# Block products for half of layer 2's w_out: seven products for eight in four of its eight units

## The chip, the cores and the metric

One core of a Trainium2 chip runs the whole program in one launch. The metric is the device time of that program in microseconds; the kernel before has a median of 2010.13 us over three runs (2009.96 to 2010.89).

## The reference, cut to what matters

Three stages in float32 over 12160 tokens (2 sequences of 6080) of width 256; both feed-forward layers widen to 2048.

```
f = lb + (1 - lb) * sigmoid(f_logit)             # gate
h[t] = f[t] * h[t-1] + (1 - f[t]) * x[t]         # scan over a sequence, y[t] = h[t]
a  = y @ w_in1;  g = a - tanh(a);         z   = g @ w_out1     # layer 1
b  = z @ w_in2;  g = max(0.01 * b, b);    out = g @ w_out2     # layer 2
```

## The kernel before, in words

**Tiles.** Tokens are cut into 12 chunks of 1024 (the last has 896), each chunk into two halves of H = 512, which are the columns of every matmul. Features lie on the 128 partitions. The work is a list of 24 items (`items`): an item is one layer over one chunk, and from item 1 on the layers take turns, so that odd items are layer 1 (of chunk c) and even items from 2 on are layer 2 (of chunk c - 1). An item has 8 units; a unit is 256 of the 2048 hidden features, as two blocks of 128.

**Precision.** Every operand is split in two float32r parts, hi (a rounded copy, made by ScalarE) and lo (the rest, by VectorE's subtraction), and every 128x128 block product is three matmuls of 512 columns: hi by hi, hi by lo, lo by hi.

**First product of a unit** (w_in, `product`, L453). The unit's 2x2 block product would take eight block products; from item 3 on it takes seven, of sums of blocks (`S1` to `S4` of the weights, `T1` to `T4` of the tokens), 21 matmuls in the PSUM banks b1, c11 and c12. Two PSUM additions on VectorE (L834, c12; L852, c22) and two copies on ScalarE (L799, c11; L821, s5) join the parts, and `act` (L481) reads the four results c11, c12, c21, c22 out to SBUF as g. In layer 1 `shrink` (L490) then subtracts the tanh. `make_forms` (L408) builds the seven token forms of an item and their hi and lo parts during the item before.

**Second product** (w_out, `emit_B`, L515). Each of the four g blocks is split (`hi`, L495, and `lo`, L500) and multiplied with two 128-wide column blocks of w_out, six matmuls for each g block and 24 for a unit, into the four banks `acc`, where all 8 units of an item add up. `sums` gives the two banks of half n; two items in turn use them crosswise.

**Order.** All engine queues are written out by hand (`manual_schedule`). The main loop (L792) takes one unit per step: in step t it issues the first product of unit t and, between its parts, the second product of unit t - 1 (`prev`), so an item's last unit is finished in step 0 of the next item. Each engine works through its queue in this order; an instruction that waits holds up all behind it on its engine. Other jobs are put into slots, four to a step (`put`, `work`): slot 4k + j of an item is place j in its step k. Such jobs are the token loads (`load_tokens`, eight DMAs of SyncE for one half of the features k), the scan of a chunk (`front`, transposes, gate and scan pieces of 256 tokens on VectorE, tanh on ScalarE; k = 0 and k = 1), the forms of the next item and `evacuate` (L527), which reads the finished sums of the item before: layer 1 by ScalarE copies (z), layer 2 by VectorE transposes straight out of PSUM (o) and four DMAs each. The slots of a layer-2 item hold both halves of the scan for the layer-1 item after it, and that item's forms; those of a layer-1 item, from its step 2 on, the forms of the next layer-2 item.

**Weights** are converted in the first items and kept in DRAM; `stream_a` (L263, two steps ahead) and `stream_b` (L272, one step ahead) bring each unit's blocks back through SyncE's queue. The pool `conv` holds the conversion's buffers, among them those of `sums_in` (L193), which adds up w_in's block sums.

Of the kernel before, what the change touches and what calls it, by code (L numbers as in the profile page):

```python
# [20 lines left out]
def tile_gated_scan_two_ffn(  # L21
# [39 lines left out]
    NPLAIN = 3  # L61
    assert [l for l, _ in items[:NPLAIN]] == [0, 0, 1]

# [8 lines left out]
    op = ctx.enter_context(tc.tile_pool(name="op", bufs=2))  # L72
# [11 lines left out]
    wb_d = [[dram.tile([P, 2, 2, DM], F32, name=f"wb{l}{u}") for u in range(NU)] for l in range(2)]  # L84

# [158 lines left out]
    wa, wb = {}, {}  # L244

    def wa_tile(key):
        wa[key] = wp.tile([P, 2, 7, P], F32R, tag="wa", name="wa")
        return wa[key]

# [13 lines left out]
    def stream_a(t):  # L263

        it, u = divmod(t, NU)
        if 0 < it < len(items):
            n = 4 if it < NPLAIN else 7
            w = wa_tile(t)[:, :, 0:n]
            nc.sync.dma_start(w.bitcast(F32), wa_d[items[it][0]][u][:, :, 0:4] if n == 4 else
                              wa_d[items[it][0]][u][:, :, 1:8])  # L270

    def stream_b(t):  # L272
        it, u = divmod(t, NU)
        if 0 < it < len(items):
            nc.sync.dma_start(wb_tile(t).bitcast(F32), wb_d[items[it][0]][u])
# [132 lines left out]
    def make_forms(it):  # L408
# [24 lines left out]
        def sub(i, a, b):  # L433
            s[i] = sp.tile([P, H], F32, tag="t", bufs=3, name="t")
# [7 lines left out]
        for i, make in (  # L442
# [8 lines left out]
            jobs += [lambda i=i: split_hi(i), lambda i=i: split_lo(i)]  # L451
        return jobs


    def product(u, bank, w, v, start=False):
        it, l, h, wt = u["it"], u["l"], u["h"], u["wa"]
# [37 lines left out]

    def hi(u, name):  # L495
        h = u["h"]
        gh = u["hi", name] = gp.tile([P, H], F32R, tag="gh", name="gh")
        nc.scalar.copy(gh[:, :h], u["g", name][:, :h])  # L498

    def lo(u, name):  # L500
        h = u["h"]
        gl = u["lo", name] = gp.tile([P, H], F32R, tag="gl", name="gl")
# [12 lines left out]
    def emit_B(u, name):  # L515
# [4 lines left out]
        first = (it, n) not in begun  # L520
        begun.add((it, n))
        for e in range(2):
            es = slice(e * P, (e + 1) * P)
            for i, (s, v) in enumerate(((0, gh), (0, gl), (1, gh))):
# [3 lines left out]
                )  # L528

    def evacuate(it, n):  # L530
# [10 lines left out]

        def o(e):
            if it == NPLAIN - 1 and n == 0:
                t = sp.tile([P, H], F32, tag="t", bufs=3, name="o")
            else:
                t = op.tile([P, H], F32, tag="o", name="o")
            nc.vector.transpose(t[:, :h], bank[e][:, :h])  # L547
# [65 lines left out]

    with tc.manual_schedule():
# [277 lines left out]
```

## Time and profile before

| | |
|---|---|
| median of the timed runs | 2010.13 us (2009.96 to 2010.89) |
| profiled execution, first to last instruction | 2007.9 us (the page gives no other time for it) |
| TensorE busy | 1982.2 us, 99% |
| VectorE busy | 1421.5 us, 71% |
| ScalarE busy | 1207.0 us, 60% |
| bytes moved by DMA | 345.68 MB, mean 172 GB/s |

TensorE is PE for matmuls and PEld for the weight loads beside them; VectorE is DVE, ScalarE is ACT, SyncE's DMA queue is SPq. L numbers are lines of the kernel. Times in rows of a timeline are microseconds from the first instruction. The duration of a matmul row is modelled and overlaps that of the next one, so the start-to-start distance tells the pace. A group of rows gives the busy time, the mean duration in ns, then the idle time of the engine ahead of these instructions and what ended it.

### The profile page before, as it was taken

Reading aid. Unit: us, or ns where it says so; the run is one execution under the profiler, and the core shown is the slowest. Engines: PE = TensorE matmul, PEld = TensorE weight load, DVE = VectorE, ACT = ScalarE, POOL = GpSimd, SP = SyncE. Lnnn points to the kernel's source line nnn. Section 1 sums busy time; section 2 is a strip of 40 time slices with the busy share of each in tenths; the row PEclk is TensorE's granted clock in tenths of the full one; section 3 lists DMA queues with packets and bytes.
Section 4 is the critical chain, followed back from the end, with each engine's and each line's share of the span. In section 5 each row is a group of like instructions: output and inputs, shape, how many; then the busy total and the mean of one; then the engine's idle time right before and its main releaser. Section 6 shows DMA issues by size and latency. Waiting matters only on the chain.

```text
span 2007.9 us, 24511 instructions
## 1 busy us (share of the span) xinstructions
PE 1982.2 (99%) x8776; PEld 1648.0 (82%) x8776; DVE 1421.5 (71%) x2259; ACT 1207.0 (60%) x2199; POOL 0.7 (0%) x6
## 2 busy tenths in 40 slices
PE   6999999999999999999999999999999999999998
PEld 4888887888888888888888888888888888889888
DVE  7989978866776775775776677677577577666443
ACT  4556656665665665666566566666566656666554
POOL 0000000000000000000000000000000000000000
PEclk8999999999999999999999999999999999999999
DMA  5556778845645554463563554555446356354352
GB/s 200 156 147 231 261 267 266 265 165 165 178 152 165 165 165 131 159 180 142 165 186 144 165 174 157 165 162 162 138 159 180 143 164 181 145 167 172 141 168 87
DMA packets 369818, 345.68 MB, mean 172 GB/s; under 512 B 273568, under 2 KB 277536, under 8 KB 369696
## 3 DMA queue, kind: packets, MB, share of 16 engines
q1 hardware_dynamic: 368048, 342.02, 52.8%
q10 hardware_dynamic: 1648, 2.10, 0.3%
q8 instruction: 69, 1.13, 0.2%
q14 instruction: 53, 0.43, 0.1%
HBM read 306.45 MB, written 37.62 MB: 171 GB/s over the span
## 4 chain that ended last, share of the span: by engine, by line
PE 94%; DVE 3%; ACT 1%; DMA 1%; issue 1%; SPq 0%; ACTq 0%; DVEq 0%
PE acc L525 49%; PE b L459 22%; PE c L459 17%; PE b L475 5%; PE c L525 1%; PE c L475 1%; DVE g L493 1%; DVE gl L503 1%; DMA raw<-in_moe_w_out_dram 0%; DVE y L346 0%; DMA rawf<-in_f_logit_dram 0%; DVE o L547 0%; DVE b L127 0%; DVE raw L138 0%; ACT g L485 0%
## 5 line engine op out<-in xcount | busy, mean ns | idle before, releaser
L525 PE MATMUL acc<-gh,wb 128*128 128x512 f32 (+1 forms) x3008 | 1017.4, 388 | 0.9 <-DVE o L547 0.5
L525 PEld LDWEIGHTS acc<-gh,wb 128*128 128x128 f32 x3008 | 565.4, 188 | 113.5 <-DVE o L547 0.9
L503 DVE TENSOR_TENSOR gl<-g,gh 128x512 fp32r<-128x512 f32 (+1 forms) x768 | 500.6, 680 | 219.7 <-ACT gh L498 211.7
L525 PE MATMUL acc<-gl,wb 128*128 128x512 f32 (+1 forms) x1504 | 583.3, 388 | 0.4 <-DVE gl L503 0.2
L498 ACT CAST gh<-g 128x512 fp32r<-128x512 f32 (+1 forms) x768 | 444.8, 615 | 86.2 <-DVE g L493 86.2
L459 PE MATMUL b<-xh,wa 128*128 128x512 f32 (+1 forms) x1344 | 493.1, 387 | 0.8 <-DVE c L852 0.6
L459 PE MATMUL c<-xh,wa 128*128 128x512 f32 (+1 forms) x1008 | 362.8, 387 | 0.0
L525 PEld LDWEIGHTS acc<-gl,wb 128*128 128x128 f32 x1504 | 282.8, 188 | 56.9 <-DVE gl L503 1.5
L487 ACT ACTIVATE g<-c 128x512 f32<-128x512 f32 (+1 forms) x272 | 154.7, 603 | 239.6 <-PE c L459 226.9
L459 PEld LDWEIGHTS b<-xh,wa 128*128 128x128 f32 x1344 | 252.3, 188 | 51.8 <-DVE c L834 1.3
L459 PE MATMUL b<-xl,wa 128*128 128x512 f32 (+1 forms) x672 | 260.0, 387 | 0.0
L485 ACT ACTIVATE g<-c 128x512 f32<-128x512 f32 (+1 forms) x244 | 139.3, 601 | 173.8 <-PE c L459 164.2
L459 PEld LDWEIGHTS c<-xh,wa 128*128 128x128 f32 x1008 | 189.2, 188 | 37.1
L852 DVE TENSOR_TENSOR c<-b,s 128x512 f32<-128x512 f32 (+1 forms) x168 | 115.0, 685 | 114.0 <-PE b L459 112.3
L459 PE MATMUL c<-xl,wa 128*128 128x512 f32 (+1 forms) x504 | 195.0, 387 | 0.0
L493 DVE TENSOR_TENSOR g<-c,g 128x512 f32<-128x512 f32 (+1 forms) x244 | 159.1, 678 | 32.1 <-ACT g L485 29.8
L799 ACT COPY c<-b 128x512 f32<-128x512 f32 (+1 forms) x168 | 94.9, 565 | 129.0 <-PE b L459 129.0
L493 DVE TENSOR_TENSOR g<-b,g 128x512 f32<-128x512 f32 (+1 forms) x140 | 95.4, 682 | 101.7 <-ACT g L485 101.7
L834 DVE TENSOR_TENSOR c<-b,s 128x512 f32<-128x512 f32 (+1 forms) x168 | 116.2, 692 | 54.4 <-PE b L459 32.0
L459 PEld LDWEIGHTS b<-xl,wa 128*128 128x128 f32 x672 | 126.1, 188 | 24.5
L485 ACT ACTIVATE g<-b 128x512 f32<-128x512 f32 (+1 forms) x140 | 83.2, 594 | 64.5 <-PE b L475 58.1
L821 ACT COPY s<-c 128x512 f32<-128x512 f32 (+1 forms) x168 | 98.0, 583 | 35.9 <-PE c L459 28.4
(96 smaller groups left out, 1267.5 us busy)
## 6 DMA issues: line engine op xcount, KB each, us to landing
wa<-wa SPq DMA_DIRECT2D x168, 896.0 KB, 5.0
wb<-wb SPq DMA_DIRECT2D x190, 512.0 KB, 5.6
wa<-st SPq DMA_DIRECT2D x24, 512.0 KB, 3.3
out_dram<-o SPq DMA_DIRECT2D x176, 64.0 KB, 1.9
wa<-wa SPq DMA_DIRECT2D x21, 512.0 KB, 6.5
rawf<-in_f_logit_dram SPq DMA_DIRECT2D x72, 128.0 KB, 5.4
rawx<-in_x_dram SPq DMA_DIRECT2D x72, 128.0 KB, 3.0
raw<-wa SPq DMA_DIRECT2D x16, 512.0 KB, 7.3
```

What stands on the lines that cost most here:

```text
L459: nc.tensor.matmul(bank[:, :h], wt[:, s, w], xx[:, v, :h], start=start and i == 0, stop=i == 2, skip_group_check=True,)
L475: nc.tensor.matmul(bank[:, :h], wt[:, s, 2 * k + j], xx[:, v[k], :h], start=i == 0, stop=i == 5,)
L485: nc.scalar.activation(g[:, :h], src[:, :h], AF.Tanh)
L487: nc.scalar.activation(g[:, :h], src[:, :h], AF.Prelu, alpha=0.01)
L493: nc.vector.tensor_tensor(g[:, :h], u["src", name][:, :h], g[:, :h], ALU.subtract)
L498: nc.scalar.copy(gh[:, :h], u["g", name][:, :h])
L503: nc.vector.tensor_tensor(gl[:, :h], u["g", name][:, :h], u["hi", name][:, :h].bitcast(F32), ALU.subtract)
L525: nc.tensor.matmul(bank[e][:, :h], w[:, j, s, es], v[:, :h], start=first and i == 0, stop=i == 2, skip_group_check=True,)
L799: nc.scalar.copy(c11[:, :h], b1[:, :h])
L821: nc.scalar.copy(s5[:, :h], c12[:, :h])
L834: nc.vector.tensor_tensor(c12[:, :h], b1[:, :h], s5[:, :h], ALU.add)
L852: nc.vector.tensor_tensor(c22[:, :h], b1[:, :h], s5[:, :h], ALU.add)
```

## The change

In nine items (`outer`: the layer-2 items 6, 8, ... 22) the second products of units 0 to 3 are no longer made by `emit_B`. They are 2x2 block products as the first one is, and run in seven block products each: c22, c21 and T4 by each unit's own weights (`own`, three matmuls each), and c11, T1, T3 and T2, whose sums meet in one bank, for two units at a time (`shared`, six matmuls). T1, T3, T2 and T4 are differences of g blocks (`diff`) with hi and lo splits of their own. A shared sum is copied out after each block (`drain`), from the second group on the running sum is first written back to the bank, and the four sums are joined (`combine`) and added to the banks' contents on the way out (`out_of`, `o`), which are now copied by ScalarE before VectorE transposes them. Steps 1 to 4 of such an item work on these units as `prev` (`sv`), steps 2 to 5 hold two shared blocks each (`grp`).

With it: w_out's block sums are made in items 4 and 5 (`sums_out`) and streamed (`stream_g`); a unit's w_in blocks come in two tiles, four in wa and three in wy (`stream_y`); the hi and lo buffers of c11 get a ring of their own (`ring`); the tag t has six buffers for three, and the pool op is gone. In the nine items the next item's tokens, scan and forms are placed anew: the first half of the scan (k = 0) goes to slots 22 to 31 of the layer-1 item before, the second (k = 1) to slots 21 to 24 and the forms, in another order, to slots 25 to 30 of the layer-2 item itself; the forms of the layer-2 item go to slots 3 to 20 of the layer-1 item before it. `sums_out`'s six VectorE operations for a pair are as in `sums_in`.

```diff
+    NWO = 4
+    W0 = 6
+    outer = [it for it, (l, c) in enumerate(items) if l == 1 and it >= W0 and it + 1 < len(items)]
...
         if 0 < it < len(items):
-            n = 4 if it < NPLAIN else 7
-            w = wa_tile(t)[:, :, 0:n]
-            nc.sync.dma_start(w.bitcast(F32), wa_d[items[it][0]][u][:, :, 0:4] if n == 4 else
-                              wa_d[items[it][0]][u][:, :, 1:8])
+            a = 0 if it < NPLAIN else 1
+            nc.sync.dma_start(wa_tile(t).bitcast(F32), wa_d[items[it][0]][u][:, :, a:a + 4])
+    def stream_y(t):
+        it, u = divmod(t, NU)
+        if NPLAIN <= it < len(items):
+            nc.sync.dma_start(wy_tile(t).bitcast(F32), wa_d[items[it][0]][u][:, :, 5:8])
...
+            w = wb_tile(t).bitcast(F32)
+            if crossed(t):
+                nc.sync.dma_start(w[:, 0], wb_d[1][u][:, 0])
+                nc.sync.dma_start(w[:, 1, :, 0:P], ws_d[u // 2][3][:, u % 2])
+            else:
+                nc.sync.dma_start(w, wb_d[items[it][0]][u])
+    def crossed(t):
+        it, u = divmod(t, NU)
+        return it in outer and u < NWO
+    def stream_g(it, g, i):
+        w = wg[it, g, i] = tp.tile([P, 2, 2, P], F32R, tag="wg", bufs=4, name="wg")
+        w = w.bitcast(F32)
+        if i:
+            nc.sync.dma_start(w, ws_d[g][i - 1])
+        else:
+            for v in range(2):
+                nc.sync.dma_start(w[:, v], wb_d[1][2 * g + v][:, 1, :, 0:P])
...
+        if spread:
+            for at in range(len(jobs) - 3, 0, -1):
+                if at in (1, 3, 5, 8, 11, 14):
+                    jobs[at:at + 2] = jobs[at + 1], jobs[at]
...
+    halves_made = [0]
+    def ring(u, name, nm):
+        if u["it"] < NPLAIN:
+            own = halves_made[0] % 5 > 2
+            halves_made[0] += nm == "l"
+        else:
+            own = name == "c11"
+        return gp.tile(
+            [P, H], F32R, tag=("c" if own else "g") + nm, bufs=2 if own else 3, name=f"g{nm}"
+        )
...
+    def diff(u, name, a, b):
+        t = u["g", name] = sp.tile([P, H], F32, tag="t", bufs=6, name="t")
+        nc.vector.tensor_tensor(t, u["g", a], u["g", b], ALU.subtract)
+    def hi_t(u, name):
+        gh = u["hi", name] = tp.tile([P, H], F32R, tag=f"{name}h", bufs=2, name=f"{name}h")
+        nc.scalar.copy(gh, u["g", name])
+    def lo_t(u, name):
+        gl = u["lo", name] = tp.tile([P, H], F32R, tag=f"{name}l", bufs=2, name=f"{name}l")
+        nc.vector.tensor_tensor(gl, u["g", name], u["hi", name].bitcast(F32), ALU.subtract)
...
-    def emit_B(u, name):
+    def emit_B(u, name, only=None):
         it, l, h, j, n = u["it"], u["l"], u["h"], int(name[1] == "1"), int(name[2]) - 1
         gh, gl, w = u["hi", name], u["lo", name], u["wb"]
         bank = sums(it, n)
-        first = (it, n) not in begun
-        begun.add((it, n))
-        for e in range(2):
+        for e in range(2) if only is None else (only,):
+            first = (it, n, e) not in begun
+            begun.add((it, n, e))
...
+    def own(u, name, n, e, j, es):
+        it, w = u["it"], u["wb"]
+        first = (it, n, e) not in begun
+        begun.add((it, n, e))
+        gh, gl = u["hi", name], u["lo", name]
+        for i, (s, v) in enumerate(((0, gh), (0, gl), (1, gh))):
+            nc.tensor.matmul(
+                sums(it, n)[e], w[:, j, s, es], v, start=first and i == 0, stop=i == 2,
+                skip_group_check=True,
+            )
...
+    def shared(it, g, i):
+        name = ("c11", "T1", "T3", "T2")[i]
+        bank, w = sums(it, 1)[1], wg[it, g, i]
+        if g == 0 and i % 2 == 0:
+            q = fp.tile([P, 2, H], F32, tag="raw", bufs=4, name="cross")
+            crosses[it, i], crosses[it, i + 1] = q[:, 0], q[:, 1]
+        for v in range(2):
+            u = pairs[it, g][v]
+            gh, gl = u["hi", name], u["lo", name]
+            for k, (s, x) in enumerate(((0, gh), (0, gl), (1, gh))):
+                nc.tensor.matmul(
+                    bank, w[:, v, s], x, start=g == 0 and v == 0 and k == 0, stop=k == 2,
+                    skip_group_check=True,
+                )
+    def drain(it, g, i):
+        bank = sums(it, 1)[1]
+        if g + 1 == NWO // 2 and i == 3:
+            q = [crosses[it, k] for k in range(4)]
+            nc.vector.tensor_tensor(q[3], bank, q[0], ALU.add)
+            return
+        nc.scalar.copy(crosses[it, i], bank)
+        if 4 * g + i > 2:
+            nc.scalar.copy(bank, crosses[it, (i + 1) % 4])
+    def combine(it):
+        q = [crosses[it, k] for k in range(4)]
+        def add(a, b):
+            return lambda: nc.vector.tensor_tensor(q[a], q[a], q[b], ALU.add)
+        crosses[it, 0, 0], crosses[it, 1, 0], crosses[it, 0, 1], crosses[it, 1, 1] = q[0], q[3], q[2], q[1]
+        return [add(2, 3), add(3, 1), add(1, 2)]
...
+        def out_of(e):
+            v = s["v", e] = sp.tile([P, H], F32, tag="t", bufs=6, name="v")
+            nc.scalar.copy(v, bank[e])
         def o(e):
-            if it == NPLAIN - 1 and n == 0:
-                t = sp.tile([P, H], F32, tag="t", bufs=3, name="o")
+            t = sp.tile([P, H], F32, tag="t", bufs=6, name="o")
+            if it in outer:
+                v = s["v", e]
+                nc.vector.tensor_tensor(v, v, crosses[it, n, e], ALU.add)
+                nc.vector.transpose(t, v)
...
+        if it in outer:
+            return [lambda i=i: out_of(i) for i in range(2)], [lambda i=i: o(i) for i in range(2)]
...
+        for g in range(NWO // 2):
+            load, jobs = sums_out(g)
+            put(4 * I + 14 + 16 * g, [load])
+            put(4 * I + 19 + 16 * g, jobs, 4 * I + 35 + 16 * g)
+        def close():
+            nonlocal tp
+            conv.__exit__(None, None, None)
+            tp = ctx.enter_context(tc.tile_pool(name="tp", bufs=2))
+        put(6 * I - 6, [close])
...
+            if it in outer:
+                jobs = []
+                if l == 0:
+                    put(base + 14, [lambda nm=nm, c=c: load_tokens(c, 1, nm) for nm in "fx"], base + 15)
+                    jobs = [f for stage in front(c, 1) for f in stage]
+                put(base + 21, jobs + make_forms(it + 1, True), base + I - 1)
+                continue
             jobs = []
+            if it + 1 in outer:
+                l0, c0 = items[it + 2]
+                if l0 == 0:
+                    put(base + 13, [lambda nm=nm, c=c0: load_tokens(c, 0, nm) for nm in "fx"], base + 14)
+                    jobs = [f for stage in front(c0, 0) for f in stage]
+                put(base + 3, make_forms(it + 1), base + 22)
+                put(base + 22, jobs, base + I)
+                continue
             if l == 0:
                 at = (base - 4, base + 2) if it > 2 else (32, 38)
                 for k in range(KD):
...
             elif it + 1 == NPLAIN:
                 put(base + 1, evacuate(it, 1))
                 put(base + 3, evacuate(it, 0))
+            elif it in outer:
+                first1, last1 = evacuate(it, 1)
+                first0, last0 = evacuate(it, 0)
+                put(base + 2, first1)
+                put(base + 4, first0)
+                put(base + 5, last1 + last0, base + 12)
             elif it + 1 < len(items):
...
+            sv = prev is not None and crossed(t - 1)
+            it, v = divmod(t, NU)
+            grp = []
+            if it in outer and 2 <= v < NWO + 2:
+                g, i = divmod(v - 2, 2)
+                if i == 0:
+                    pairs[it, g] = us_s[2 * g:2 * g + 2]
+                grp = [(it, g, 2 * i), (it, g, 2 * i + 1)]
             if t < NC:
                 u = unit(t)
...
+                if sv:
+                    hi(prev, "c22")
...
+            if sv:
+                diff(prev, "T1", "c12", "c11")
+                diff(prev, "T3", "c22", "c12")
+                diff(prev, "T2", "c22", "T1")
+                lo(prev, "c22")
+            elif prev:
...
+            stream_y(t + 1)
             if prev:
                 prev["wb"] = wb[t - 1]
+            if grp:
+                shared(*grp[0])
+            if sv:
+                hi(prev, "c21")
+                if grp:
+                    hi_t(prev, "T1")
+                diff(prev, "T4", "c21", "T2")
+                lo(prev, "c21")
+                if grp:
+                    hi(prev, "T4")
+                    lo_t(prev, "T1")
+            elif prev:
                 emit_B(prev, "c11")
                 hi(prev, "c12")
                 hi(prev, "c22")
                 shrink(prev, "c21")
                 lo(prev, "c12")
+            if grp:
+                drain(*grp[0])
             if u:
                 product(u, c12, S1, T1, start=True)
                 s5 = sp.tile([P, H], F32, tag="s5", name="s5")
                 nc.scalar.copy(s5[:, :h], c12[:, :h])
...
+            if sv:
+                if grp:
+                    lo(prev, "T4")
+                else:
+                    hi(prev, "T4")
...
+            if sv:
+                own(prev, "c22", 1, 0, 1, slice(0, P))
+                own(prev, "c21", 0, 0, 0, slice(0, P))
+                if not grp:
+                    hi_t(prev, "T1")
+                hi_t(prev, "T3")
+                hi_t(prev, "T2")
+                if not grp:
+                    lo(prev, "T4")
+                    lo_t(prev, "T1")
+                else:
+                    lo_t(prev, "T3")
+            if grp:
+                shared(*grp[1])
+            if prev and not sv:
+                emit_B(prev, "c12", 0 if grp else None)
                 lo(prev, "c21")
-            else:
+            elif not prev:
                 todo.pop(0)()
             if u:
                 hi(u, "c11")
-            if prev:
-                emit_B(prev, "c22")
+            if prev and not sv:
+                emit_B(prev, "c22", 0 if grp else None)
...
                 lo(u, "c11")
+            if grp:
+                drain(*grp[1])
+                if grp[1][1:] == (NWO // 2 - 1, 3):
+                    put(NS * t + 3, combine(it), NS * t + 6)
             work(NS * t + 2)
+            if it in outer and v < NWO:
+                g, i = divmod(v, 2)
+                stream_g(it, g, 2 * i)
+                stream_g(it, g, 2 * i + 1)
...
+                if sv:
+                    if not grp:
+                        lo_t(prev, "T3")
+                    lo_t(prev, "T2")
...
+            if sv:
+                own(prev, "T4", 0, 1, 0, slice(P, 2 * P))
+            elif prev:
+                if grp:
+                    emit_B(prev, "c12", 1)
+                    emit_B(prev, "c22", 1)
                 emit_B(prev, "c21")
```

## Rows read from the trace of the kernel before

**Rows 1.** The page's head and part 1: busy us (share of span), instructions.

```profile
span 2007.9 us, 24511 instructions
...
PE 1982.2 (99%) x8776; PEld 1648.0 (82%) x8776; DVE 1421.5 (71%) x2259; ACT 1207.0 (60%) x2199; POOL 0.7 (0%) x6
```

**Rows 2.** The page's part 4, the chain that ended last, by engine.

```profile
PE 94%; DVE 3%; ACT 1%; DMA 1%; issue 1%; SPq 0%; ACTq 0%; DVEq 0%
```

**Rows 3.** Waits of TensorE from 300 to 1960 us: us, times, longest.

```profile
PE b L459 <- DVE c L852: 0.6, 1, 0.6
PE acc L525 <- DVE o L547: 0.5, 1, 0.5
```

**Rows 4.** Windows of items 10 and 11: length, busy us, PEclk, DMA share.

```profile
868.90:950.50 81.60, 81.60 (x361) 67.57 (x360) 54.40 (x88) 51.38 (x96) 0.00 (x0) 1.00 0.46 155
950.50:1032.10 81.60, 81.60 (x361) 67.57 (x360) 59.30 (x93) 48.29 (x87) 0.00 (x0) 1.00 0.55 168
```

**Rows 5.** Groups by line and shape, all the span: count, busy, mean ns.

```profile
L503 DVE TENSOR_TENSOR gl<-g,gh 128x512 fp32r<-128x512 f32 x704 | 463.1, 685 | 194.5 <-ACT gh L498 187.3
...
L498 ACT CAST gh<-g 128x512 fp32r<-128x512 f32 x704 | 411.4, 620 | 79.7 <-DVE g L493 79.6
...
L799 ACT COPY c<-b 128x512 f32<-128x512 f32 x152 | 86.7, 570 | 117.1 <-PE b L459 117.1
...
L547 DVE STREAM_TRANSPOSE o<-acc 128x512 f32<-128x512 f32 x44 | 31.2, 710 | 11.9 <-PE b L459 7.5 <-DMA out_dram<-o 4.2 <-PE acc L525 0.2
```

**Rows 6.** Timeline of ScalarE, item 10: start, us, engine, line, operation.

```profile
913.30 0.59 ACT L821 COPY s<-c 128x512 f32<-128x512 f32 x1 [0.35 <-PE c L459]
913.79 0.62 ACT L427 CAST xh<-y 128x512 fp32r<-128x512 f32 x1
914.31 0.60 ACT L487 ACTIVATE g<-c 128x512 f32<-128x512 f32 x1
```

**Rows 7.** Timeline of VectorE, item 10, step 3 (from 899.50).

```profile
904.53 0.70 DVE L834 TENSOR_TENSOR c<-b,s 128x512 f32<-128x512 f32 x1 [0.36 <-PE b L459]
905.14 1.28 DVE L503 TENSOR_TENSOR gl<-g,gh 128x512 fp32r<-128x512 f32 x2
906.34 0.69 DVE L387 SCALAR_TENSOR_TENSOR tx<-tf,tx 128x512 f32<-128x512 f32 x1
907.86 0.69 DVE L852 TENSOR_TENSOR c<-b,s 128x512 f32<-128x512 f32 x1 [0.83 <-PE b L459]
...
909.07 0.74 DVE L398 TENSOR_TENSOR_SCAN y<-tf,carry,tx 128x256 f32<-128x256 f32 x1
909.85 2.32 DVE L398 TENSOR_TENSOR_SCAN y<-tf,y,tx 128x256 f32<-128x256 f32 x3
```

**Rows 8.** Timeline of TensorE, the same step: S2, S3, next A11.

```profile
903.58 0.39 PE L459 MATMUL b<-xh,wa 128*128 128x512 f32 x1
...
906.98 0.39 PE L459 MATMUL b<-xh,wa 128*128 128x512 f32 x1
...
909.70 0.39 PE L459 MATMUL b<-xh,wa 128*128 128x512 f32 x1
```

**Rows 9.** Windows, one step: step 1 of item 11.

```profile
960.70:970.90 10.20, 10.20 (x46) 8.45 (x45) 7.68 (x13) 5.63 (x11) 0.00 (x0) 1.00 0.76 170
```

**Rows 10.** Timeline of SyncE's queue: one k's token loads.

```profile
871.67 5.56 SPq L288 DMA_DIRECT2D rawf<-in_f_logit_dram  x4
877.27 2.81 SPq L288 DMA_DIRECT2D rawx<-in_x_dram  x4
```

**Rows 11.** The page's part 6, DMA issues: count, KB, us to landing.

```profile
wa<-wa SPq DMA_DIRECT2D x168, 896.0 KB, 5.0
```

**Rows 12.** Groups by line and shape: a conversion's addition, 1024 wide.

```profile
L215 DVE TENSOR_TENSOR f<-raw 128x1024 f32<-128x1024 f32 x8 | 9.7, 1218 | 0.0
```

More of the change, by code (lines that the diff above doesn't have):

```diff
@@ L84, in tile_gated_scan_two_ffn @@
     wb_d = [[dram.tile([P, 2, 2, DM], F32, name=f"wb{l}{u}") for u in range(NU)] for l in range(2)]
+    ws_d = [[dram.tile([P, 2, 2, P], F32, name=f"ws{g}{i}") for i in range(4)] for g in range(NWO // 2)]
     A11, A22, A12, S1, S2, S3, S4 = range(7)
@@ L241, in sums_in, with sums_out, f0, s0 @@
         return f0, [s0, s1, s2, s3, s4, s5]
-    wa, wb = {}, {}
+    def sums_out(g):
+        s = {}
+        sh = [P, 4, 2 * P]
+        def f0():
+            s["raw"] = cv.tile(sh, U64, tag="raw", bufs=2, name="raw").bitcast(F32).rearrange(
+                "p (n j) (s q) -> p n j s q", n=2, s=2
+            )
+            for i in range(2):
+                nc.sync.dma_start(s["raw"][:, i], wb_d[1][2 * g + i])
+        def s0():
+            t = cv.tile(sh, F32, tag="c", bufs=2, name="f")
+            s["f"] = t.rearrange("p (n j) (e q) -> p n j e q", n=2, e=2)
+            nc.vector.tensor_tensor(
+                t.rearrange("p (n j) q -> p n j q", n=2), s["raw"][:, :, :, 0], s["raw"][:, :, :, 1], ALU.add
+            )
+        def s1():
+            f = s["f"]
+            r = s["s"] = cv.tile(sh, F32, tag="c", bufs=2, name="s").rearrange("p a (n q) -> p a n q", n=2)
+            nc.vector.tensor_tensor(r[:, 0], f[:, :, 1, 1], f[:, :, 0, 1], ALU.add)
+            nc.vector.tensor_tensor(r[:, 1], f[:, :, 1, 0], f[:, :, 1, 1], ALU.subtract)
+        def s2():
+            f, r = s["f"], s["s"]
+            nc.vector.tensor_tensor(r[:, 2], r[:, 0], f[:, :, 1, 0], ALU.subtract)
+            nc.vector.tensor_tensor(r[:, 3], f[:, :, 0, 0], r[:, 2], ALU.subtract)
+        def s3():
+            s["w"] = cv.tile([P, 2, 2, 4, P], F32R, tag="st", name="st").rearrange(
+                "p x y z q -> p (x y z) q"
+            ).rearrange("p (a n h) q -> p a n h q", a=4, n=2)
+            nc.scalar.copy(s["w"][:, :, :, 0], s["s"])
+        def s4():
+            nc.vector.tensor_tensor(
+                s["w"][:, :, :, 1], s["s"], s["w"][:, :, :, 0].bitcast(F32), ALU.subtract
+            )
+        def s5():
+            for i in range(4):
+                nc.sync.dma_start(ws_d[g][i], s["w"][:, i].bitcast(F32))
+        return f0, [s0, s1, s2, s3, s4, s5]
+    wa, wy, wb, wg = {}, {}, {}, {}
     def wa_tile(key):
-        wa[key] = wp.tile([P, 2, 7, P], F32R, tag="wa", name="wa")
+        wa[key] = wp.tile([P, 2, 4, P], F32R, tag="wa", name="wa")
         return wa[key]
+    def wy_tile(key):
+        wy[key] = wp.tile([P, 2, 3, P], F32R, tag="wy", bufs=2, name="wy")
+        return wy[key]
     def wb_tile(key):
@@ L433, in sub @@
         def sub(i, a, b):
-            s[i] = sp.tile([P, H], F32, tag="t", bufs=3, name="t")
+            s[i] = sp.tile([P, H], F32, tag="t", bufs=6, name="t")
             nc.vector.tensor_tensor(s[i][:, :h], a(), b(), ALU.subtract)
@@ L501, in lo @@
         h = u["h"]
-        gl = u["lo", name] = gp.tile([P, H], F32R, tag="gl", name="gl")
+        gl = u["lo", name] = ring(u, name, "l")
         nc.vector.tensor_tensor(
@@ L852, in tile_gated_scan_two_ffn @@
                 nc.vector.tensor_tensor(c22[:, :h], b1[:, :h], s5[:, :h], ALU.add)
+                if sv:
+                    if not grp:
+                        lo_t(prev, "T3")
+                    lo_t(prev, "T2")
+                    lo(u, "c11")
                 product(u, c12, S4, B22)
```

35 lines of the change are left out of this document (19 added, 16 removed).

## Prediction

> **What bounds the kernel now.** The page comes first: TensorE is busy for 1982.2 of 2007.9 us [rows 1], and the chain that ended last is 94% TensorE [rows 2]. A busy TensorE can still be a waiting one, so the waits come next: from 300 to 1960 us TensorE waited twice, 1.1 us in all [rows 3]. The other engines keep up everywhere. The two stages show the pace: an item of layer 2 and one of layer 1 both last 81.60 us, TensorE busy throughout, at granted clock 1.00 [rows 4]. An item has 8 steps of 45 matmuls, so a step is 10.20 us and a matmul 81.60/360 = 0.2267 us. While nothing else ends late, time is matmuls by 0.2267 us, and removing twelve removes 2.72 us.
>
> The span is 2007.9 us. The timed runs have a median of 2010.13, 2.2 us more, which the change does not touch. I work with differences and put them on 2010.1.
>
> **What goes.** In nine items, units 0 to 3 issued 24 second-product matmuls each, 96 in all. Now each issues 9 (`own`: c22, c21, T4), and two pairs share four blocks of 6 (`shared`): 36 + 48 = 84. Twelve fewer in nine items: 108 x 0.2267 = 24.5 us. Nothing else on TensorE changes in number. If no engine is late, the time is 2010.1 - 24.5 = 1985.6, the floor.
>
> Within an item it is uneven. Steps 0, 6 and 7 keep 45 matmuls; step 1 has 30 (6.80 us), steps 2 to 4 have 42 (9.52 us), step 5 has 57 (12.92 us).
>
> **What comes: VectorE and ScalarE, steps 1 to 4.** A lo split averages 685 ns, a hi split 620, a copy to PSUM 570 [rows 5]. These are not the price in a queue. On ScalarE, starts lie 913.30, 913.79, 914.31 [rows 6], so 0.49 to 0.52 us apart; on VectorE two lo splits begin at 905.14 and the next operation at 906.34 [rows 7], 0.60 apart. I take 0.52 and 0.60.
>
> Such a step has 13 VectorE operations (7 lo splits, 4 differences, 2 additions): 7.8 us. ScalarE has 13 as well, plus two evacuations in step 1 and 2, 3 and 4 drain copies in steps 2, 3 and 4: 15, 15, 16 and 17 operations, 7.8 to 8.8 us. Steps 2 to 4 have 9.52 us, so the work fits; step 1 has 6.80, so both engines fall about 1 us behind and carry it into step 2.
>
> Does that reach TensorE? Only where a matmul comes due first. The latencies are in rows: an addition starts 0.95 us after its product's first matmul (903.58 to 904.53), and the c22 addition 0.88 us (906.98 to 907.86) [rows 7, 8]. I place both queues in program order, step 1's first matmul at zero. ScalarE starts hi c22 at 0.0, the c11 copy 0.88 (its product's end), z 1.40, act c21 1.92, hi c21 2.44, s5 2.96, hi T4 3.48, z 4.0, act c11 4.5 and hi T1 5.0. VectorE starts T4's difference at 2.55 (act c21 ends 2.52), lo c21 3.15, the c12 addition 3.75 (s5 ends 3.55), lo T4 4.36, lo T1 5.66 (hi T1 ends 5.62) and the c22 addition 6.26, ending 6.95, due 7.48 (A22 of step 2). From there it has no gap: nine starts on, step 2's lo c21 begins 11.66 and ends 12.35, due 12.47. T4's difference ends 11.75, so its hi split starts 11.79 and the drain 12.31, ending 12.9, due 12.92 (second shared block); s5 follows at 12.81 and the c12 addition at 13.45, ending 14.15, due 14.31 (S3). In step 3 the rhythm is recovered by 0.3 to 1 us. So no stall by the rows, but margins of 0.02 to 0.16 us over some twenty operations. Bounds: 0, and 1.6 us if each of those operations costs 0.08 more (mean duration instead of spacing). I take 0.2, near the rows.
>
> **A wait that is added.** T2's hi tile has two buffers. Unit 2's hi split of T2 stands in step 3 before the shared block that still reads unit 0's, so it waits for that block: ScalarE stops about 1.4 us. Behind it stand hi of c11, two drain copies, the two activations and the next step's c11 copy, for which TensorE waits: that copy then ends at 28.3 on my clock, due 29.27. Taken at nothing; without that 1.0 us of cover it costs up to 0.4.
>
> **The pile in step 6.** Half a scan (k=1) and all input forms, 30 jobs, now stand three to a slot in the last ten slots of these items. At slot 23 VectorE has two transposes, a multiply and an addition, at slot 24 a multiply, four scan pieces (909.07 to 912.17: 0.78 each [rows 7]) and an addition, and then the lo split of c12, for which TensorE waits. From step 5's c22 addition this queue runs 7.6 us and the split ends 5.04 us into step 6, due 4.99. Bounds 0 and 0.7 (0.09 more for each of eight). I take 0.1.
>
> **The next item, layer 1.** Each of four outputs costs an addition besides the transpose (710 ns [rows 5]), 1.3 us together, at slots 5, 6, 8 and 10, and the forms start at slot 3. VectorE was busy 7.68 of 10.20 us in such a step [rows 9]; ten operations of a plain step at 0.60 are 6.0, and steps 1 and 2 add two outputs and two or three form operations: 9.8 and 10.4 us. In program order step 1's c22 addition stands behind lo c11 (ends 8.05), a form (8.65) and an output (9.95) and ends at 10.6, due 10.88; in step 2 the two shrinks start 0.35 and 1.08, a form 1.7, an output 2.3, the shrink of c21 3.6, and the lo split of c12 ends at 4.9, due 4.99. Bounds 0 and 2.5 (16 and 17 operations at mean duration). I take 0.2. The four copies out of PSUM go to ScalarE, 48.29 of 81.60 us busy [rows 4]: nothing.
>
> **Moved and small edits.** The other half scan (k=0) stands one job to a slot in the layer-1 item's last ten slots, where a c22 addition may be 1.8 us late (907.86 + 0.69 against 910.38 [rows 7, 8]); one 1.6 us scan job fits. Token loads are no more, but stand elsewhere: eight take 5.56 + 2.81 = 8.4 us of SP's queue [rows 10]. In step 3 the two g loads, then stream_a and stream_y of step 4, wait behind them. The last is issued about 31.0, lands 5 us later by the wa row [rows 11], and is due 40.8; the first g load has 2.5 us. Nothing, while transfers stay under 7 us. wa in two pieces moves the same bytes. The new weight sums run in items 4 and 5 beside plain steps, per pair two additions of 1.22 us [rows 12] and four quarter-size ones: 0 to 2 us once, I take 0.3. Rings, renamed tags and the later pool close: 0, at most 0.5 either way, hidden by the same slack.
>
> **Sum.** -24.5 + 9 x (0.2 + 0.1 + 0.2) + 0.3 = -19.7, so 1990.4; I say 1990.
>
> **A rule that speaks against it.** The Trainium skill, "VectorE: DVE Perf Modes", section "The DRAIN you can't avoid", says that the next operation does not start until the pipe has emptied. Taken as full durations end to end, it is the second rival. Here starts lie 0.60 apart under durations of 0.685, so the trace does not bear it out for independent operations.
>
> **Rivals.**
> 1. *Part of the gain is given back in the crossed steps.* The margins of step 2 fail: in-order queues of ScalarE and VectorE wait for each other (T4's difference waits for act c21, its hi split for the difference, the drain for that). Two of the 2.72 us are lost per item: 2010.1 - 24.5 + 18 = 2003.6. For it: both engines over 80% busy in steps 2 to 4, with margins under 0.2 us. Against: VectorE already stood idle for 194.5 us ahead of its lo splits, nearly all of it for ScalarE [rows 5], and TensorE did not wait for that.
> 2. *Slower: VectorE's operations lie at full duration, not 0.60.* Mechanism: where each operation waits for another engine's result, its start follows the end of the one before. Then the crossed steps lose 0.9 us, step 6 0.7, and the layer-1 item after it 2.5 (eight such items): 9 x 1.6 + 8 x 2.5 - 24.5 = +9.9, so 2020. It turns slower once 2.72 us are lost per item, about 0.66 us a start. Against: the pair of lo splits at 905.14 waits for ScalarE's tiles and is 0.60 apart [rows 7].
> 3. *A transfer is late.* The g load or wy behind the token loads lands 2 us late in each item: 9 x 2 us, 2004 with the rest. For: 8.4 us of SP's queue before it. Against: layer 2's DMA share is 0.46 [rows 4].
> 4. *It does not do what it says*, twelve matmuls not gone: excluded by counting them in the diff.
>
> **How the numbers follow.** Forecast 0.62 (its own range 1985.6 to 1996), first rival 0.17, second 0.11, third 0.06, anything else 0.04. The floor is hard, so the range starts at 1985; it ends at 2005, past the first and third rivals, leaving out the second, half of the rest and some upper tails. 0.2% is 4 us, about what can be told from no change. Faster (under 2006.1) holds the forecast and most of rivals 1 and 3: 0.82. Same: their tails and the weak form of the second, 0.07. Slower: 0.11.
>
> **What would show it.** 108 fewer matmuls, and TensorE's step times 6.8, 9.5, 9.5, 9.5, 12.9 us in a layer-2 item of 78.9 us. Right: TensorE waits in the waits view stay under 1 us per item. The first rival shows as waits of second-product matmuls for ScalarE's bank copies or VectorE's lo splits in step 2; the second as starts 0.69 apart and waits in layer-1 steps 1 and 2; the third as waits for wg or wy. My forecast is wrong if layer-2 items last over 80 us, or layer-1 items over 82.

## The result, and the profile after

The changed kernel takes 1994.2 us (1994.13 to 1994.56), the kernel before 2010.5 us on the same chip: ratio 0.992, 95% interval 0.9906 to 0.9934. The forecast was 1990 in a range of 1985 to 2005: the direction holds, and so does the mechanism of the gain, which is 16.3 us where 20 were forecast and 24.5 were the most there could be. One sign of being wrong that the prediction named did come: layer-1 items last over 82 us, by 0.06.

The page after: the span, part 1 and the head of part 4.

```profile
span 1992.2 us, 25301 instructions
...
PE 1963.4 (99%) x8668; PEld 1623.5 (81%) x8668; DVE 1611.2 (81%) x2595; ACT 1331.7 (67%) x2444; POOL 0.7 (0%) x6
...
PE 93%; DVE 4%; DMA 1%; ACT 1%; issue 1%; SPq 0%; ACTq 0%; DVEq 0%
```

108 matmuls fewer (8668 for 8776 [rows 1]) and 15.7 us less span. VectorE is now 81% busy instead of 71%, ScalarE 67% instead of 60%, and the chain still runs 93% through TensorE [rows 2]. The page does not say where the rest of the 24.5 us went; the times of the items do. An item lasts from the c11 copy of its step 0 to that of the next item's; here these copies of items 10, 11 and 12 on ScalarE's timeline (start, us, line, operation):

```profile
867.32 0.57 ACT L1013 COPY c<-b 128x512 f32<-128x512 f32 x1 [0.62 <-PE b L542]
...
946.61 0.57 ACT L1013 COPY c<-b 128x512 f32<-128x512 f32 x1 [0.92 <-PE b L542]
...
1028.67 0.57 ACT L1013 COPY c<-b 128x512 f32<-128x512 f32 x1 [0.62 <-PE b L542]
```

So item 10 (layer 2) lasts 79.29 us and item 11 (layer 1) 82.06, where both were 81.60 [rows 4]. The same distances for all items:

| items | before | after | twelve matmuls or none | lost |
|---|---|---|---|---|
| layer 2, items 6 to 18 (seven) | 81.60 | 79.28 | 78.88 | 0.40 each |
| layer 2, items 20, 22 | 81.53, 80.94 | 78.98, 78.43 | 78.81, 78.22 | 0.17, 0.21 |
| layer 1, items 7 to 19 (seven) | 81.60 (item 9: 82.75) | 82.06 | 81.60 | 0.46 each |
| layer 1, item 21 (448 columns) | 73.75 | 74.84 | 73.75 | 1.1 |
| item 3 | 81.97 | 83.63 | 81.97 | 1.7 |
| item 5 | 81.60 | 82.43 | 81.60 | 0.8 |

Added up: 2.8 + 0.4 + 3.2 + 1.1 + 1.7 + 0.8 = 10.0 us lost. The profile of before has a single wait in item 9 (82.75 us; the 0.5 us for an output in [rows 3] and the matmuls behind it) that the one after has not, and it starts item 3 0.1 us later: 24.5 - 10.0 + 1.2 = 15.7, the difference of the spans.

Where these waits are is hardly seen in TensorE's matmul rows, whose durations are modelled: from 300 to 1960 us they show 2.8 us. A wait for an operand stands at the weight load in front (PEld). That view for the same stretch, us in total, times, longest:

```profile
PEld acc L632 <- DVE gl L598: 6.1, 16, 0.6
PEld b L542 <- DVE c L1113: 3.7, 10, 1.0
PEld acc L662 <- ACT cross L674: 2.2, 9, 0.2
PEld b L542 <- DMA wy<-wa: 1.8, 1, 1.8
PEld acc L646 <- DVE gl L598: 1.7, 9, 0.2
```

`gl` at L632 is the lo split of c12 that `emit_B` waits for, in step 6 of the layer-2 items and in step 2 of the layer-1 items (and once in item 3, as before); L1113 is the c22 addition, in step 1 of the layer-1 items above all; L662 and L646 are the shared and own blocks of step 2. The same view of the kernel before shows 4.3 us in seven places, five of them in item 3 and late in both kernels.

### The profile page after: what moved, and what is told of

It is laid out like the page before. It is cut to its first block, busy times and chain, and to the rows that moved or that the text cites. A ratio compares the mean times of both kernels' runs of the same rounds, so it can differ in the third digit from the quotient of the medians.

```text
span 1992.2 us, 25301 instructions
## 1 busy us (share of the span) xinstructions
PE 1963.4 (99%) x8668; PEld 1623.5 (81%) x8668; DVE 1611.2 (81%) x2595; ACT 1331.7 (67%) x2444; POOL 0.7 (0%) x6
## 4 chain that ended last, share of the span: by engine, by line
PE 93%; DVE 4%; DMA 1%; ACT 1%; issue 1%; SPq 0%; ACTq 0%; DVEq 0%
PE acc L632 39%; PE b L542 22%; PE c L542 17%; PE acc L662 5%; PE b L558 5%; PE acc L646 4%; PE c L632 1%; DVE g L576 1%; DVE gl L598 1%; PE c L558 1%; DMA raw<-in_moe_w_out_dram 0%; DMA wy<-wa 0%; DVE y L424 0%; DMA rawf<-in_f_logit_dram 0%; DVE b L130 0%
## 5 line engine op out<-in xcount | busy, mean ns | idle before, releaser
L632 PE MATMUL acc<-gh,wb 128*128 128x512 f32 (+1 forms) x2432 | 822.3, 388 | 1.0 <-DVE o L713 0.5
L632 PEld LDWEIGHTS acc<-gh,wb 128*128 128x128 f32 x2432 | 457.1, 188 | 91.5 <-DVE o L713 1.0
L632 PE MATMUL acc<-gl,wb 128*128 128x512 f32 (+1 forms) x1216 | 472.7, 389 | 0.5 <-DVE gl L598 0.4
L632 PEld LDWEIGHTS acc<-gl,wb 128*128 128x128 f32 x1216 | 228.6, 188 | 50.3 <-DVE gl L598 6.6
L542 PE MATMUL b<-xh,wy 128*128 128x512 f32 (+1 forms) x672 | 260.4, 388 | 1.6 <-DMA wy<-wa 1.3
L542 PE MATMUL b<-xh,wa 128*128 128x512 f32 (+1 forms) x672 | 234.2, 388 | 0.8 <-DVE c L1113 0.8
L542 PE MATMUL c<-xh,wa 128*128 128x512 f32 (+1 forms) x672 | 232.8, 387 | 0.0
L1113 DVE TENSOR_TENSOR c<-b,s 128x512 f32<-128x512 f32 (+1 forms) x168 | 113.6, 676 | 55.3 <-PE b L542 54.3
L542 PEld LDWEIGHTS b<-xh,wy 128*128 128x128 f32 x672 | 126.2, 188 | 28.0 <-DMA wy<-wa 1.8
L542 PEld LDWEIGHTS b<-xh,wa 128*128 128x128 f32 x672 | 126.1, 188 | 28.1 <-DVE c L1113 3.7
L542 PE MATMUL b<-xl,wa 128*128 128x512 f32 (+1 forms) x336 | 130.0, 387 | 0.0
L542 PE MATMUL b<-xl,wy 128*128 128x512 f32 (+1 forms) x336 | 130.0, 387 | 0.0
L542 PE MATMUL c<-xh,wy 128*128 128x512 f32 (+1 forms) x336 | 130.0, 387 | 0.0
```

The source lines that it names most:

```text
L542: nc.tensor.matmul(bank[:, :h], wt[:, s, w], xx[:, v, :h], start=start and i == 0, stop=i == 2, skip_group_check=True,)
L632: nc.tensor.matmul(bank[e][:, :h], w[:, j, s, es], v[:, :h], start=first and i == 0, stop=i == 2, skip_group_check=True,)
L1113: nc.vector.tensor_tensor(c22[:, :h], b1[:, :h], s5[:, :h], ALU.add)
```

## The experiments

My theory: the gain is 108 matmuls at 0.2267 us, less a few short waits, each at a place in an in-order queue whose margin is used up. Rival B: VectorE (or ScalarE) simply has too much work in these items, wherever it stands. Rival C: the new placement of scan, forms and loads carries part of the gain or loss. On the chips of these runs the kernel before takes 2010.1 to 2010.3 us; ratios are to that.

**Placement without block products.** `crossed`, `grp`, `out_of` and the added sums are tied to an empty list, `joined`, in place of `outer`:

```diff
-        return it in outer and u < NWO
+        return it in joined and u < NWO
...
-            if it in outer and 2 <= v < NWO + 2:
+            if it in joined and 2 <= v < NWO + 2:
```

> Everything of the change but the block products themselves: the second products run as eight block products everywhere, with the new places of loads, scan, forms, the split wa/wy tiles and the weight sums. My theory (the gain is 108 matmuls, the placement gives nothing by itself): layer-2 items at 81.6 to 81.8 us, layer-1 items at 81.6, total 2011 to 2014 us, a little over before because of the late first wy load (1.5 us) and the weight sums in item 5 (0.8 us). Rival C (the new placement carries part of the gain): under 2008 us.

2013.75 us, ratio 1.0017 (1.0008 to 1.0027). Layer-1 items 81.60, layer-2 items 82.0. Rival C falls for the gain and holds for the loss: the placement by itself costs 3.5 us, in item 3 (1.5), in item 5 (0.8) and in step 6 of seven layer-2 items (0.40 each, where 0 to 0.2 were expected), less what the profile of before had lost in item 9 and ahead of item 3. So the pile in step 6 holds TensorE up without any block product. It does so more than in the changed kernel, it seems because step 5 has 45 matmuls and not 57: the c22 addition of step 5 starts 1.7 us ahead of step 6 here and 3.1 us there, so VectorE begins the pile later (read from the timelines of item 10; no run isolates it). The lo split is late seven times there, 0.5 us each at the weight load; the eighth wait of this row is the one in item 3.

```profile
PEld acc L633 <- DVE gl L599: 4.0, 8, 0.5
```

**Five items instead of nine**, same placement (`joined` holds items 14 to 22).

> Block products only in items 14 to 22 (five instead of nine), the placement unchanged. My theory: each crossed pair of items is worth 2.72 - 0.40 - 0.46 = 1.9 us net, so four fewer cost 7 to 8 us: 2001 to 2002.5 us, uncrossed layer-2 items at 81.6 to 81.8 us, crossed ones still at 79.3. Rival C: not in proportion, the uncrossed items also under 81 us.

2003.59 us, ratio 0.9967 (0.9955 to 0.9979). The total missed my band by 1.1 us. The uncrossed layer-2 items take 82.0 as above, not 81.6 to 81.8, so a pair of items is worth 163.6 - 161.35 = 2.25 us by these distances, four pairs 9.0; and item 21 takes 75.72 for 74.84, 0.9 us more that have nothing to do with the number of items (last section). The gain goes with the number of crossed items; layer-1 items after uncrossed ones are back at 81.60.

**One more VectorE operation in step 2, and in step 4.** The lo split of c22 is made twice; the other kernel has `v == 4`.

```diff
                 lo(prev, "c22")
+                if v == 2:
+                    nc.vector.tensor_tensor(
+                        prev["lo", "c22"], prev["g", "c22"], prev["hi", "c22"].bitcast(F32), ALU.subtract
+                    )
```

> One more VectorE operation of 0.60 us in step 2 of each of the nine items (the lo split of c22 made twice, same values). My theory (margins in the queue decide, and step 2 has none left: VectorE runs without a gap up to the c12 addition): TensorE is held up by 0.5 to 0.7 us more per item, layer-2 items 79.8 to 80.0 us, total 4 to 6 us over the changed kernel's 1994.2. Rival B (VectorE's overall share, 81%, leaves room for 0.6 us in 79): no change, under 1 us in all.

> The same extra VectorE operation, but in step 4 instead of step 2. My theory (by step 4 the queue has 0.3 to 1 us to spare): 0 to 0.2 us per item, total within 1.5 us of 1994.2. If any added VectorE work in the crossed steps costs its full length (saturation, rival B in its strong form): 5.4 us more, as much as in step 2.

In step 2: 2001.01 us, 6.8 more, 0.8 above my band; layer-2 items 80.0, 0.72 more each. That is the whole operation: it writes the tile that the split ahead of it has just written and starts 0.71 after that one, not 0.60, and with its own 0.60 VectorE's queue is 0.72 longer (VectorE's timeline of item 10: starts at 888.57, 889.28, 889.89). Own blocks wait for lo of c22 and c21:

```profile
PEld acc L646 <- DVE gl L598: 6.0, 9, 0.7
...
PEld acc L646 <- DVE gl L1020: 3.5, 9, 0.4
```

In step 4: 1997.81 us, 3.6 more where at most 1.5 were expected; layer-2 items 79.6, 0.31 more each, and 0.9 again from item 21. So the place matters, as the theory says, and rival B in both forms falls (0 or the full length alike in both steps). But my margin of step 4 was too wide. TensorE does not wait for VectorE itself here: VectorE makes T4's difference later, so ScalarE makes its hi split later, and behind that stands ScalarE's write-back into the bank (L676), for which the second shared block waits 0.4 us:

```profile
PEld acc L662 <- ACT acc L676: 3.8, 9, 0.4
```

**The first wy load earlier.** `stream_y` of the loop's first unit moves from the head of the loop to slot 88, ahead of the w_out loads.

> Only the first wy load of the main loop is issued earlier, before the loads of w_out that hold SyncE's queue for 7.3 us. My theory: the 1.5 us wait of TensorE at the start of item 3 (c products done, wy not landed) goes, item 3 falls from 83.6 to 82.1 us, total 1.5 us lower, about 1992.7. Rival: the load is late because the DMA engines are full there, then the wait stays above 1 us.

1994.93 us (1992.09 to 1996.11; the profile is of the slowest), item 3 at 86.1: no gain in the median. Why the four times lie 4 us apart is open. In the changed kernel the load is issued at 295.16, behind two w_out loads that hold SyncE's queue for 7.26 us (timeline of SyncE's queue), and TensorE stands from 300.58 to 302.30 (timeline of TensorE):

```profile
286.58 7.26 SPq L338 DMA_DIRECT2D wb<-wb  x2
...
295.16 0.61 SPq L328 DMA_DIRECT2D wy<-wa  x1
```

```profile
300.58 0.39 PE L542 MATMUL c<-xh,wa 128*128 128x512 f32 x1
302.30 0.50 PE L542 MATMUL b<-xh,wy 128*128 128x512 f32 x1 [1.34 <-DMA wy<-wa]
```

With the load at 274.99 that wait is gone, but the third one, issued in step 1, now comes too late: SyncE first issues twelve output DMAs of item 2, 10.22 us, and only then this load at 317.07 (SyncE's queue; below it TensorE's wait).

```profile
274.99 0.65 SPq L328 DMA_DIRECT2D wy<-wa  x1
...
306.13 10.22 SPq L717 DMA_DIRECT2D out_dram<-o  x12
...
317.07 0.61 SPq L328 DMA_DIRECT2D wy<-wa  x1
```

```profile
PE b L542 <- DMA wy<-wa: 2.6, 1, 2.6
```

In the changed kernel the same load is issued at 315.86 and nothing waits for it: TensorE, held up before, comes to it later. Neither reading foresaw this: it is one queue with two places to fall behind. The 2.6 us cost more than themselves: right behind them the granted clock is 0.50, 1.2 GHz, in the first of these two windows (the third number from the end), as in no other run at this place, after TensorE had stood idle; ten matmuls are done there, sixteen in the next.

```profile
323.50:326.90 3.40, 3.40 (x10) 2.65 (x9) 2.50 (x4) 1.14 (x2) 0.00 (x0) 0.50 1.02 352
326.90:330.30 3.40, 3.40 (x16) 2.81 (x16) 1.86 (x3) 1.12 (x2) 0.00 (x0) 0.99 1.04 394
```

**Outputs apart.**

```diff
-                put(base + 5, last1 + last0, base + 12)
+                for at, f in zip((5, 7, 10, 13), last1 + last0):
+                    put(base + at, [f])
```

> The four output jobs of a layer-2 item stand at slots 5, 7, 10 and 13 of the next item instead of 5, 6, 8 and 10, so none stands ahead of the lo split of c12 in step 2. My theory: layer-1 items fall from 82.06 to 81.6 to 81.75 us, total 2.5 to 3.7 us lower, about 1991. Rival B (VectorE has too much work in these steps, wherever it stands): under 1 us.

1990.41 us, ratio 0.9904 (0.9887 to 0.9921); layer-1 items 81.66, item 21 73.84. The waits for c12's lo split fall from 16 to 8, the seven of step 6 and the one in item 3:

```profile
PEld acc L632 <- DVE gl L598: 2.8, 8, 0.5
```

**Scan and forms one slot earlier**: `put(base + 20, ...)` for `base + 21`.

> The scan half and the forms of the nine items begin one slot earlier (slot 20), so that one scan piece pair instead of two stands at the head of step 6. My theory: the wait for lo of c12 in step 6 (0.17 us) goes, layer-2 items 79.1 us, total 1.0 to 1.5 us lower. Rival: VectorE is then held up in step 5 instead (the tokens' transposes wait for their load), no gain or a loss.

1993.77 us, ratio 0.9916 (0.9901 to 0.993). Layer-2 items 79.05, 0.23 less, as expected; in the total it does not show, since item 21 took 0.9 us longer (last section) and the start 0.6.

**T2's hi split behind the shared block**, so that nothing queues behind its wait:

```diff
                 hi_t(prev, "T3")
-                hi_t(prev, "T2")
+                if not grp:
+                    hi_t(prev, "T2")
...
+            if sv and grp:
+                hi_t(prev, "T2")
             if grp:
                 drain(*grp[1])
```

> The hi split of T2 stands behind the second shared block in ScalarE's queue, so that in step 3 nothing stands behind its wait for that block's buffer. My theory (that wait is covered by the 1 us of slack before the c11 copy): layer-2 items unchanged within 0.1 us, total within 1 us of 1994.2. Rival: the wait is part of the 0.40 us per item, which then falls by 0.1 or more.

1994.24 us, layer-2 items 79.23 to 79.34: no difference. The added wait, 0.65 us of ScalarE in item 10 of the changed kernel, is covered.

**All mended**: outputs apart, scan one slot earlier, the first wy load earlier and every further one at the head of its step, the weight sums four slots later.

```diff
             it, v = divmod(t, NU)
+            stream_y(t + 1)
...
             stream_a(t + 2)
-            stream_y(t + 1)
...
-            put(4 * I + 19 + 16 * g, jobs, 4 * I + 35 + 16 * g)
+            put(4 * I + 23 + 16 * g, jobs, 4 * I + 39 + 16 * g)
```

> All places where the changed kernel still waits, mended together: outputs at slots 5, 7, 10, 13; scan and forms one slot earlier; the first wy load earlier and every further wy load at the head of its step in SyncE's queue, ahead of the output DMAs; the weight sums four slots later. My theory (each wait is a place in a queue, so each mend keeps its own gain): layer-2 items 79.05 us, layer-1 items 81.65, item 3 at 82.0, item 5 at 81.6, total 1985 to 1988 us. Rival B (VectorE has too much work; moving it only moves the wait): layer-1 or layer-2 items stay at 82.0 or 79.3 and the total at 1990 or above.

1986.71 us (1986.57 to 1986.78), ratio 0.9882 (0.9866 to 0.9899): layer-2 items 79.05, layer-1 items 81.66, item 3 81.97, item 5 81.60. It beats both kernels. Of the waits at weight loads that the change brought, these remain, all in step 2, and one of 0.2 us in item 21:

```profile
PEld acc L662 <- ACT cross L674: 2.1, 9, 0.2
PEld acc L646 <- DVE gl L598: 1.7, 9, 0.2
```

Each mend kept its gain by the item times, so the work was not too much; it stood in the wrong order.

## Why the prediction was right, and where its sizes were off

**Removed matmuls.** As counted: 108, at an unchanged pace. Steps 1 to 4 of item 10 after the change (windows from first matmul to first matmul; length, then busy us of TensorE, weight loads, VectorE, ScalarE):

```profile
876.64:883.44 6.80, 6.80 (x31) 5.63 (x30) 5.68 (x10) 6.77 (x14) 0.00 (x0) 1.00 0.56 164
883.44:893.15 9.71, 9.71 (x43) 7.73 (x42) 9.23 (x16) 8.78 (x17) 0.00 (x0) 1.00 0.82 260
893.15:902.67 9.52, 9.52 (x43) 7.88 (x42) 7.99 (x14) 8.49 (x17) 0.00 (x0) 1.00 0.70 184
902.67:912.19 9.52, 9.52 (x43) 7.88 (x42) 8.10 (x14) 9.23 (x18) 0.00 (x0) 1.00 0.98 234
```

Forecast were 6.80 and three times 9.52: step 2 loses 0.19 us, the others nothing.

**Steps 1 to 4: 0.2 taken, 0.17 measured** (79.05 less 78.88 once the pile is relieved). VectorE's timeline of item 10, step 1 from 876.64 (c12 and c22 additions), step 2's lo of c21 and c12 addition:

```profile
880.39 0.69 DVE L1073 TENSOR_TENSOR c<-b,s 128x512 f32<-128x512 f32 x1
...
882.89 0.68 DVE L1113 TENSOR_TENSOR c<-b,s 128x512 f32<-128x512 f32 x1
...
888.30 0.69 DVE L598 TENSOR_TENSOR gl<-g,gh 128x512 fp32r<-128x512 f32 x1
...
890.11 0.69 DVE L1073 TENSOR_TENSOR c<-b,s 128x512 f32<-128x512 f32 x1
```

From 876.64 these start at 3.75, 6.25, 11.66 and 13.47; placed by hand were 3.75, 6.26, 11.66 and 13.45. The spacing of 0.60 holds through both steps, though most of these operations take another engine's result. That is what the second rival denied, and its 2020 us did not come; the waits in layer-1 steps 1 and 2, which it also named, did, but not by its cause. The Trainium skill, "VectorE: DVE Perf Modes", section "The DRAIN you can't avoid", has the next operation wait until the pipe is empty. Read as full durations end to end the trace does not agree: starts 0.60 apart under durations of 0.685. But this reading, the prediction's too, leaves out what the same paragraph says last, that an operation which is not held starts earlier. With that the trace agrees. Step 2 is indeed the place without a margin: lo c21 ended at 12.35 (due 12.47) and the drain at 12.89 (due 12.92), both as forecast, and TensorE still lost 0.19 us. So "no stall by the rows" was wrong, and the 0.2 that was taken beside it was a guess that came out; the pile shows why.

**The added wait for T2: nothing, and nothing was measured** (T2's split moved: the same item times).

**The pile in step 6: 0.1 taken, 0.23 measured.** Right place and instruction, the size within its bounds of 0 to 0.7, and the queue was forecast almost to the point: step 6 of item 10 starts at 925.12, and the lo split of c12 (the first of the two below) ended at 930.10, 4.98 into it (forecast 5.04), just when it was due (4.99). Yet TensorE lost 0.21 us there. Timelines of VectorE, of the weight loads and of TensorE, one after the other:

```profile
929.42 1.28 DVE L598 TENSOR_TENSOR gl<-g,gh 128x512 fp32r<-128x512 f32 x2
...
929.65 0.19 PEld L632 LDWEIGHTS acc<-gh,wb 128*128 128x128 f32 x1
930.15 0.19 PEld L632 LDWEIGHTS acc<-gl,wb 128*128 128x128 f32 x1 [0.32 <-DVE gl L598]
...
929.88 0.39 PE L632 MATMUL acc<-gh,wb 128*128 128x512 f32 x1
930.16 0.50 PE L632 MATMUL acc<-gl,wb 128*128 128x512 f32 x1
```

The weight load of a matmul that does not wait starts 0.23 us ahead of it (929.65 for 929.88). The one that needs the split starts 0.05 us after the split's end, and its matmul only then. So in this trace an operand is due some 0.2 us before its matmul, while every due time of the prediction is the matmul's own start. Margins of 0.02 to 0.16 us were none: this step of the prediction failed in step 2, here, and in the next item alike.

**The layer-1 item: 0.2 taken, 0.46 measured, 1.1 in item 21.** This is the term that was mis-sized most, and its part of the forecast is wrong by the prediction's own sign (items over 82 us). The due times above are one reason; the other is a delay that had no price. The prediction gave the four copies out of PSUM to ScalarE at nothing, since ScalarE was 59% busy there [rows 4]. But one stands at slot 4, ahead of act c21, in ScalarE's timeline of item 11, step 1 (from 955.93):

```profile
956.35 0.59 ACT L704 COPY v<-acc 128x512 f32<-128x512 f32 x1
956.83 0.60 ACT L1013 COPY c<-b 128x512 f32<-128x512 f32 x1
957.35 0.60 ACT L704 COPY v<-acc 128x512 f32<-128x512 f32 x1
957.83 0.62 ACT L568 ACTIVATE g<-b 128x512 f32<-128x512 f32 x1
```

It moves act c21 from 1.62 into the step, where it stood before the change, to 1.90. The shrink of c21 on VectorE starts 0.65 behind it, so at 2.55 instead of 2.27, and as VectorE has only one gap of 0.16 from there to the lo split of c12, the delay is carried. VectorE's timeline, the shrink of c21, the first output and the c22 addition in step 1, then the third output, the shrink of c21 and the lo splits in step 2 (from 966.16):

```profile
958.48 0.69 DVE L576 TENSOR_TENSOR g<-b,g 128x512 f32<-128x512 f32 x1 [1.13 <-ACT g L568]
...
960.28 0.68 DVE L710 TENSOR_TENSOR v<-v,cross 128x512 f32<-128x512 f32 x1
961.00 0.71 DVE L711 STREAM_TRANSPOSE o<-v 128x512 f32<-128x512 f32 x1
...
966.15 0.65 DVE L1113 TENSOR_TENSOR c<-b,s 128x512 f32<-128x512 f32 x1
...
968.77 0.69 DVE L710 TENSOR_TENSOR v<-v,cross 128x512 f32<-128x512 f32 x1
969.49 0.71 DVE L711 STREAM_TRANSPOSE o<-v 128x512 f32<-128x512 f32 x1
970.12 0.65 DVE L576 TENSOR_TENSOR g<-b,g 128x512 f32<-128x512 f32 x1
970.70 1.27 DVE L598 TENSOR_TENSOR gl<-g,gh 128x512 fp32r<-128x512 f32 x2
```

An output takes 1.36 us, not 1.3: the transpose reads what the addition wrote and starts 0.03 to 0.04 after its end. The c22 addition ends at 10.87 into step 1 (forecast 10.6, due 10.88). Step 2's lo split of c12 ends at 5.2 into its step, forecast 4.9, due 4.99, and TensorE's timeline shows the matmul at 971.43 that should follow 0.23 behind:

```profile
971.08 0.39 PE L632 MATMUL acc<-gh,wb 128*128 128x512 f32 x1
971.43 0.50 PE L632 MATMUL acc<-gl,wb 128*128 128x512 f32 x1
```

By matmul starts against 0.2267 us each, TensorE loses 0.16 of the 0.46 behind the c22 addition and 0.27 at this split. An engine with idle time over an item still delays what queues behind the added instruction. That a second engine without gaps hands the delay on is read from these rows; no run takes ScalarE's copy away. The experiment with the outputs apart leaves it where it is (act c21 at 1.89, shrink of c21 at 2.54 there too) and moves outputs on VectorE alone, and the loss falls to 0.06: what is shown is that VectorE's order decides, and not how much of the 0.46 is the copy's.

**Weight sums: 0.3 taken, 0.8 measured**, in item 5, where outputs of item 4 must leave the bank; four slots later it is gone.

**Token loads and wa in two pieces: nothing taken, 1.7 measured.** It was not the token loads, which I had placed in SyncE's queue, but the first wy loads, whose place in the queue at the end of the plain items I did not look up. The third rival (a late transfer) had the mechanism but another place.

**Sum.** Terms priced: 9 x 0.5 + 0.3 = 4.8; measured for the same: 2.8 + 0.4 + 3.2 + 1.1 + 0.8 = 8.3, and 1.7 unpriced, less the 1.2 that before's profile had lost itself. That 1.2 was in no forecast, so it is luck that the total lies no further off. The first rival's signs came in step 2 (the rows of L662 and L646), its 2 us per item did not: 0.19 there, 0.40 in all. Two slips in the sums change nothing: item 23 is layer 2, so eight layer-1 items follow and not nine (4.6 for 4.8); and the third rival "with the rest" is 2008, not 2004, by the prediction's own terms, so the range did not reach past it.

## What to carry to other kernels

Where one engine is the bound and the others follow in written order, price an added instruction by the place it takes: how long until the bound engine needs what is queued behind it, on its own engine and on the next. Where the bound engine is TensorE, count that time to the weight load and not to the matmul; it was 0.2 us here, more than the margins that the forecast stood on. The busy share of an engine over an item says little: one more VectorE operation, 0.72 us in its queue, cost 0.72 in one step and 0.31 two steps on. And place each queue from its first instruction, the DMA queue at the border between two phases included.

## What the runs showed of the hardware that was not expected

The 448-column matmuls of item 21 settle at one of two paces. Steps of 45 take 9.12 us before, in the changed kernel (first fence: c11 copies on ScalarE, steps 5 and 6) and in six experiments, but 9.30 from step 4 on in the runs with the scan earlier (second fence), five items, and the extra operation in step 4, at granted clock 1.00 and without a wait. What decides is open; all three had the 0.6 us wait in step 2 before, but so had the changed kernel.

```profile
1800.37 0.52 ACT L1013 COPY c<-b 128x448 f32<-128x448 f32 x1 [0.24 <-PE b L542]
...
1809.49 0.52 ACT L1013 COPY c<-b 128x448 f32<-128x448 f32 x1 [0.75 <-PE b L542]
```

```profile
1799.98 0.52 ACT L1013 COPY c<-b 128x448 f32<-128x448 f32 x1 [0.28 <-PE b L542]
...
1809.28 0.52 ACT L1013 COPY c<-b 128x448 f32<-128x448 f32 x1 [0.79 <-PE b L542]
```

The start before item 3 took 296.6 to 297.6 us in these profiles: the granted clock alternates between 1.2 and 2.4 GHz (0.50 and 1.00) from about 15 us until 40 to 53 us, not always alike. That scatter is of the size of single mends, which were therefore read from item times.
